# Third chunk's rows from a product on chip, scores ahead of the first gate product, and a new hand-written order, in a fused attention, expert and mixer kernel

## The chip, the cores and the metric

The kernel runs on one core of a Trainium2 chip. The metric is the device time of one execution in microseconds (us), the median of several runs. TensorE is called PE here, VectorE DVE, ScalarE ACT, GpSimd POOL, and SyncE SP; SP issues nearly all DMAs.

## What is computed

Three layers, one behind the other, on a batch of 2 with 768 positions, 8 heads of 40 and so 320 columns:

```
# 1. a gated linear recurrence (per batch and head)
m_new = max(f[t] + m, i[t]); C = exp(f[t] + m - m_new) * C + exp(i[t] - m_new) * outer(v[t], k[t])
n     = exp(f[t] + m - m_new) * n + exp(i[t] - m_new) * k[t]
y[t]  = sigmoid(o[t]) * (C @ q[t]) / max(|n . q[t]|, 1)
# 2. four experts of causal attention (head size 64), the best two of four per position, weighted
a = softmax(mask(q @ k.T / 8)); out += weight * (a @ v @ wo)
# 3. a mixer: over positions (768 -> 256 -> 768), then over columns (320 -> 1536 -> 320)
u = x + (relu(x.T @ w_tok1) @ w_tok2).T;  out = u + relu(u @ w_ch1) @ w_ch2
```

## The kernel before

The recurrence is worked in 12 chunks of 128 positions (6 of each batch, n = 0 to 11). A first stage on DVE scans the gates of all heads at once: `gates` (L322 on) makes running sums `fl`, then `av`, a running maximum `mt`, and from these, with ACT's help, the split operands `lt` and, in `m_ends`, `msp`, both in the tile `ms`. It does so in three pieces of two chunks. The gates of the first two chunks come by two DMAs (`gates0`), the others by one of 512 KB (`gates1`), which SP issues as its fourth.

For each chunk, `m_rows` lays the row maxima of four heads into a tile `rt` of 128 x 512 (four such tiles; chunks from 2 on use the last two in turn). Chunks 0 and 1 get theirs by a product of `msp` with a selection out of `smlt`, on DVE as one multiplication or on ACT as four activations; the later chunks fill the tile once with ones and zeros (`copy`) and then have SP write rows into it by two DMAs out of `msp`. `m_products` multiplies `lt` with `rt` on the PE, with a mask product (`negb`, `identb`) in front for the first four chunks; `m_gates` takes the exponential on ACT into `e`; `m_whole` makes the score products `kv` x `kv`; `m_scores` multiplies both on DVE into `e` (L587) and makes `vs` for the carried state. `m_carry` makes the carry's weights `w` by a product with `mc`, `m_intra` multiplies `e` and `w` with values and carried state (`cb`), divides (`dn`, `x`), and transposes x into `xt`, `m_update` renews the state `cc`, `cb`. Every second chunk is then projected (`p_qk`, `p_v`) with the weights `wh`, `wl`. Attention (`a_scores` to `a_tail`) and the mixer follow.

Nothing is scheduled at run time: the table `ORDER` (L45 on) is a list of some 1,500 numbers. A number x runs the next step of part x // 5 on engine "PAVGS"[x % 5]; a step states what must have been done and which buffers it takes. A negative number -k puts k fillers on the PE (products of `still`, zeros in bf16 of 128 columns). Each engine executes its instructions in that order and waits for what they need, so the table sets the order on every engine and, for copies and multiplications that several engines can do, which one does them. The 8 PSUM banks are handed round.

Of the kernel before, what the change touches and what calls it, by code (L numbers as in the profile page):

```python
# [39 lines left out]
EARLY = 4  # L40
STOP = -1000
# [14 lines left out]
    937, 422, 524, 895, 187, 508, 432, 900, STOP, 560, 917, 187, 440, 488, 936, 896, 387, 440, 561, 901, 1482, 530,  # L56
# [1175 lines left out]
```

## Time and profile before

| | us |
|---|---|
| median of 3 runs | 334.23 (334.22 to 334.96) |
| the profiled execution | 334.46 |
| its span, first to last instruction | 332.7 |

| engine | busy us | share of the span |
|---|---|---|
| PE | 326.1 | 98% |
| DVE | 243.1 | 73% |
| ACT | 179.4 | 54% |
| POOL | 43.3 | 13% |

A busy share is an average over stages: DVE is nearly always busy up to about 180 us and half idle behind, the PE is busy throughout. Products on the PE overlap, so that each one's duration is longer than the step from its start to the next one's start.

### The profile page before, as it was taken

To read this page: it belongs to the slowest core of one execution; us is meant where nothing else is said; L and a number is where in the kernel's file an instruction comes from. 1 tells how busy PE (TensorE), PEld (TensorE's weight loads), DVE (VectorE), ACT (ScalarE), POOL (GpSimd) and SP (SyncE) were. 2 spreads that over 40 slices of the span, in tenths; PEclk is the share of its full clock that TensorE was granted. 3 is DMA by queue.
4 is the path that set the end of the run, shared out by engine and by line. 5 is a ranking of instruction groups with operands and counts; after the bars stand their busy time and mean duration, and the time that the engine had idled before them with its cause. 6 is when DMAs were issued, how large, how long until landed. Compare 5 with 4: busy or idle time off the path is not lost.

```text
span 332.7 us, 7751 instructions
## 1 busy us (share of the span) xinstructions
PE 326.1 (98%) x3034; PEld 293.8 (88%) x3034; DVE 243.1 (73%) x674; ACT 179.4 (54%) x453; POOL 43.3 (13%) x82
## 2 busy tenths in 40 slices
PE   8999999999989999999999999999999999999995
PEld 7779989898888989988899899999889989889985
DVE  4999999999999999999997636543535886411413
ACT  7997769787938886678685513311213442211110
POOL 4232443031421000011120010000000000000000
PEclk9999999999999999999999999999999999999999
DMA  7962844540300354121011502000101200100302
GB/s 228 394 225 97 304 157 153 216 155 13 144 0 3 128 175 144 49 87 41 2 42 48 164 12 89 0 0 2 47 0 41 87 1 2 39 2 0 104 16 79
DMA packets 10300, 29.05 MB, mean 87 GB/s; under 512 B 1272, under 2 KB 3224, under 8 KB 10264
## 3 DMA queue, kind: packets, MB, share of 16 engines
q1 hardware_dynamic: 10120, 28.54, 24.8%
q8 instruction: 24, 0.39, 0.5%
q14 instruction: 12, 0.10, 0.1%
q10 hardware_dynamic: 144, 0.02, 0.0%
HBM read 26.50 MB, written 1.97 MB: 86 GB/s over the span
## 4 chain that ended last, share of the span: by engine, by line
PE 57%; DVE 32%; ACT 4%; issue 3%; DMA 2%; SPq 0%; POOL 0%; DVEq 0%; POOLq 0%; ACTq 0%
PE bank L195 52%; DVE am L864 3%; PE bank L881 3%; DVE e L587 3%; DVE tf L477 3%; DVE tf L474 2%; DMA gt<-in_dram 2%; DVE cw L219 1%; DVE w L222 1%; DVE tf L472 1%; DVE xt L677 1%; ACT am L870 1%; DVE x L222 1%; PE bank L625 1%; DVE q L763 1%
## 5 line engine op out<-in xcount | busy, mean ns | idle before, releaser
L195 PE MATMUL bank<-ut,cw 128*128 128x512 f32 x288 | 72.4, 395 | 0.0
L195 PE MATMUL bank<-cw,h 128*128 128x320 f32 x432 | 70.6, 310 | 0.0
L195 PEld LDWEIGHTS bank<-cw,h 128*128 128x128 f32 x432 | 66.0, 188 | 2.7 <-issue 0.2
L1044 ACT ACTIVATE h<-bank 128x512 fp32r<-128x512 f32 x36 | 21.6, 600 | 78.4 <-PE bank L195 78.3
L195 PEld LDWEIGHTS bank<-ut,cw 128*128 128x128 f32 x288 | 52.6, 188 | 9.8
L1046 DVE SCALAR_TENSOR_TENSOR h<-bank,h 128x512 fp32r<-128x512 f32 x36 | 24.8, 689 | 48.4 <-ACT h L1044 48.4
L870 ACT ACTIVATE am<-am,mn 128x128 f32<-128x128 f32 (+5 forms) x48 | 32.1, 671 | 11.0 <-DVE mn L867 6.6
L864 DVE CUSTOM_DVE_ANT_0 am<-bank,mk 128x384 f32<-128x384 f32 (+3 forms) x64 | 30.6, 500 | 0.8 <-PE bank L195 0.7
L195 PE MATMUL bank<-xt,wh 128*128 128x256 f32 x144 | 26.6, 290 | 0.0
L881 PE MATMUL bank<-ident,am 128*128 128x128 f32 x168 | 24.8, 275 | 0.0
L195 PE MATMUL bank<-ks,q 64*128 64x384 f32 (+2 forms) x192 | 22.4, 343 | 1.1 <-DVE q L763 1.0
L469 ACT ACTIVATE tf<-raw 128x384 f32<-128x384 f32 (+1 forms) x32 | 17.1, 535 | 11.4 <-DVE cw L219 6.0
L216 ACT COPY atr<-bank 128x384 f32<-128x384 f32 (+3 forms) x53 | 22.2, 442 | 2.0 <-PE bank L881 1.9
L195 PEld LDWEIGHTS bank<-xt,wh 128*128 128x128 f32 x144 | 21.8, 189 | 1.0 <-issue 0.2
L195 PE MATMUL bank<-atr,vg 128*64 128x128 f32 x336 | 22.2, 277 | 0.0
L881 PEld LDWEIGHTS bank<-ident,am 128*128 128x128 f32 x168 | 19.4, 140 | 1.8 <-issue 0.3
L195 PEld LDWEIGHTS bank<-atr,vg 128*64 128x64 f32 x336 | 18.4, 137 | 2.1 <-issue 0.6
L195 PEld LDWEIGHTS bank<-ks,q 64*128 64x128 f32 x192 | 15.8, 185 | 4.9 <-DVE q L763 1.2
L477 DVE SCALAR_TENSOR_TENSOR tf<-raw,minus,tf 128x384 uint32<-128x384 uint32 (+1 forms) x32 | 19.1, 595 | 0.2
L474 DVE SCALAR_TENSOR_TENSOR tf<-raw,tf 128x384 uint32<-128x384 uint32 (+1 forms) x32 | 17.5, 556 | 0.3
L1070 DVE TENSOR_TENSOR u<-bank,u 128x320 f32<-128x320 f32 x24 | 11.0, 486 | 8.5 <-PE bank L195 8.5
L587 DVE TENSOR_TENSOR e<-bank,e 128x512 f32<-128x512 f32 x24 | 16.2, 682 | 0.1
(160 smaller groups left out, 601.5 us busy)
## 6 DMA issues: line engine op xcount, KB each, us to landing
kv<-in_dram SPq DMA_DIRECT2D x11, 848.0 KB
raw<-in_dram SPq DMA_DIRECT2D x20, 384.0 KB
raw<-in_dram SPq DMA_DIRECT2D x13, 320.0 KB
os<-in_dram SPq DMA_DIRECT2D x4, 480.0 KB
out_dram<-u SPq DMA_DIRECT2D x12, 160.0 KB
raw<-in_dram SPq DMA_DIRECT2D x3, 386.0 KB
kv<-in_dram SPq DMA_DIRECT2D x1, 512.0 KB
gt<-in_dram SPq DMA_DIRECT2D x1, 512.0 KB
```

What stands on the lines that cost most here:

```text
L195: PE.matmul(o, lt, r, start=first, stop=last)
L216: (A.copy if e == "A" else V.tensor_copy)(o, i)
L469: A.activation(t, w[:, :, 1].bitcast(F32), AF.Copy, scale=2.0 ** -112)
L474: V.scalar_tensor_tensor(u, w[:, :, 0], 29, u, op0=OP.logical_shift_right, op1=OP.bitwise_or)
L477: V.scalar_tensor_tensor(t.bitcast(U32), w[:, :, 1], minus.bitcast(U32), u, op0=OP.bitwise_and, op1=OP.bitwise_or)
L587: V.tensor_mul(EE[n, u], PS[n][u], EE[n, u])
L864: V.tensor_tensor_reduce(a[:, b0 * 128:b1 * 128], s["p", e, ci], mks, -0.125, 3e38, OP.add, OP.min, s["mn"][:, ci, e:e + 1])
L870: A.activation(a[:, 0:w], a[:, 0:w], AF.Exp, bias=s["mn"][:, z, e:e + 1], scale=-1.0, accum_out=s["sm"][:, 0, e:e + 1])
L881: PE.transpose(pt[:, k - b0], a[:, k * 128:(k + 1) * 128], ident)
L1044: A.activation(h[0], p1, AF.Relu)
L1046: V.scalar_tensor_tensor(h[1], p1, 0.0, f32(h[0]), op0=OP.max, op1=OP.subtract)
L1070: V.tensor_add(uo(b, i), ACC[h, n // 4][n % 4], uo(b, i))
```

## The change

Three rules are changed, and the table is a new one. The constant `DIRECT = 3` lets chunk 2 get its rows by the product too, so that the DMAs begin with chunk 3. `m_products` waits for the chunk before it by its own mark ("pd") and no longer by the count that the carry's product shares. `m_whole` no longer waits for the gate product of its chunk, only for the score products of the chunk before, so that scores can stand in front. A step of `a_tail` waits for its neighbour's. The program gains one line, so that every line number behind it is one higher.

```diff
+DIRECT = 3
 ORDER = [
-    12, -19, 65, 4, 12, 256, 196, 12, 16, 17, 11, 61, 65, 12, 111, -49, 65, 12, 12, 86, 49, 9, 109, 12, 71, 12, 16,
+    4, 12, 256, -19, 65, 12, 12, 65, 16, 17, 11, -18, 75, 12, 9, 12, 61, 112, 12, 65, 147, 115, 115, 71, 115, 12,
...
     def m_rows(n):
         b, c = divmod(n, NCH)
         free = (("mg", n - 2),) if n > 3 else ()
-        if n > 1 and (n < 4 or c < 2):
+        if n >= DIRECT and (n < DIRECT + 2 or c < 2):
             yield on("AV", "sml", *free)
             copy(plan.eng, rt(n), sel(n, True))
-        if n > 1:
-            yield on("S", ("msp", c), *free, *((("rti", n - 1),) if n > 2 else ()))
+        if n >= DIRECT:
+            yield on("S", ("msp", c), *free, *((("rti", n - 1),) if n > DIRECT else ()))
...
-                yield on("P", "idb", *((("mg", n - 1),) if n else ()), take=["bank"])
+                yield on("P", "idb", *((("pd", n - 1),) if n else ()), take=["bank"])
...
-        yield on("P", ("kv" if n else "kq", n), ("pd", n), take=["bank"] * 2)
+        yield on("P", ("kv" if n else "kq", n), *((("ps", n - 1),) if n else ()), take=["bank"] * 2)
...
-        yield on("AV", take=["big"] * (1 - i % 2))
+        yield on("AV", *((("up", b, i - 1),) if i % 2 else ()), take=["big"] * (1 - i % 2))
```

By the built programs, the fillers go from 80 (19, 49, 2, 2, 8) to 55 (19, 18, 11, 3, 2, 1, 1), POOL makes 19 `vs` instead of 14 and 7 `x` instead of 3, and DVE that many fewer.

On the PE, at the first gate products, behind the 49 fillers (`rt_86` and `rt_87` hold the rows of chunks 0 and 1, `kv_72` is the first chunk's load), stood:

```order
L195 MATMUL bank<-rt_86,ms 128x512 x2
L195 LDWEIGHTS identb
L195 MATMUL bank<-negb,identb 128x512
L195 MATMUL bank<-kv_72 128x128 x8
L195 LDWEIGHTS identb
L195 MATMUL bank<-negb,identb 128x512
L195 MATMUL bank<-rt_87,ms 128x512 x2
```

There stands now, on the PE behind 18 fillers:

```order
L196 MATMUL bank<-kv_72 128x128 x8
L196 MATMUL bank<-rt_86,ms 128x512 x2
L196 LDWEIGHTS identb
L196 MATMUL bank<-negb,identb 128x512
L196 LDWEIGHTS identb
L196 MATMUL bank<-negb,identb 128x512
L196 MATMUL bank<-rt_87,ms 128x512 x2
L196 MATMUL bank<-rt_87,mc 128x512
```

The scores of chunk 0 are now in front of its gate product, and the carry product of chunk 1 follows its gate product at once. (A row with x8 on two halves of the array is 16 records in the profile.)

On DVE, from the end of the first gates' piece to the second piece (`mp` belongs to the carry, the first `gt` scan to the gates of chunks 2 and 3), stood:

```order
L420 SCALAR_TENSOR_TENSOR mp<-mpf,smlt,mp 128x1
L327 SCALAR_TENSOR_TENSOR gt<-zz,gt 128x256
L219 TENSOR_TENSOR gt<-gt 128x256
L331 TENSOR_SCALAR zz<-gt 128x2
L334 SCALAR_TENSOR_TENSOR mh<-zz,mh,gt 128x256
L222 TENSOR_TENSOR vs<-kv_72,e 128x164
L587 TENSOR_TENSOR e<-bank,e 128x512
```

There stands now, on DVE at the same place:

```order
L421 SCALAR_TENSOR_TENSOR mp<-mpf,smlt,mp 128x1
L223 TENSOR_TENSOR rt_87<-smlt,ms 128x512
L328 SCALAR_TENSOR_TENSOR gt<-zz,gt 128x256
L599 TENSOR_SCALAR mc<-smlt,mp 128x128
L220 TENSOR_TENSOR gt<-gt 128x256
L332 TENSOR_SCALAR zz<-gt 128x2
L223 TENSOR_TENSOR vs<-kv_72,e 128x164
L335 SCALAR_TENSOR_TENSOR mh<-zz,mh,gt 128x256
L588 TENSOR_TENSOR e<-bank,e 128x512 x2
```

DVE now makes the rows of chunk 1 in front of the second gates' scan, and `mc` behind it, both ACT's work before.

On ACT, from the first rows on (`hs` is a half of the split operands, `w` the carry's weights), stood:

```order
L379 ACTIVATE rt_86<-ms,smlt 128x128 x4
L379 ACTIVATE rt_87<-ms,smlt 128x128 x4
L548 ACTIVATE e<-bank 128x512 x2
L352 ACTIVATE hs<-mh,smlt 128x256
L337 ACTIVATE hs<-gt,smlt 128x256
L596 ACTIVATE mc<-smlt,mp 128x128
L548 ACTIVATE e<-bank 128x512 x2
L606 ACTIVATE w<-bank 128x512
```

There stands now, on ACT at the same place (`rt_88` holds the third chunk's rows):

```order
L380 ACTIVATE rt_86<-ms,smlt 128x128 x4
L549 ACTIVATE e<-bank 128x512 x4
L353 ACTIVATE hs<-mh,smlt 128x256
L338 ACTIVATE hs<-gt,smlt 128x256
L607 ACTIVATE w<-bank 128x512
L380 ACTIVATE rt_88<-ms,smlt 128x128 x4
L405 ACTIVATE os<-os 128x960
```

The rows of chunk 1 have left ACT, the exponentials of chunks 0 and 1 stand in a row in front of the second piece, and the third chunk's rows are made behind it. On SP, the first of the weight loads (`raw`, 386 KB) stood in front of the second half of the first `kv`, and stands behind the third `kv` now; in front of the fourth `kv` SP issues the loads of the second half of the first kv, kv 1, os, kv 2, wo, two raw and the rows of chunk 3, where it was raw, kv, kv 1, os, kv 2, raw, the rows of chunk 2, os.

## Rows read from the trace of the kernel before

**Rows 1.** The page's busy times: engine, us, share of the span, instructions

```profile
PE 326.1 (98%) x3034; PEld 293.8 (88%) x3034; DVE 243.1 (73%) x674; ACT 179.4 (54%) x453; POOL 43.3 (13%) x82
```

**Rows 2.** Busy us by stage: from:to, length, PE, weight loads, DVE, ACT, POOL

```profile
8.08:21.63 13.55, 12.97 (x193) 9.77 (x191) 12.96 (x33) 12.81 (x32) 4.10 (x7) 1.00 0.90 346
21.63:192.00 170.37, 168.83 (x1992) 152.90 (x1992) 160.46 (x496) 127.11 (x343) 33.30 (x55) 1.00 0.31 107
192.00:329.30 137.30, 137.28 (x784) 124.94 (x782) 65.19 (x134) 33.69 (x67) 2.14 (x3) 1.00 0.08 26
```

**Rows 3.** Timeline of the PE, start: start us, us, what, count [idle before]

```profile
3.99 4.16 PE L195 MATMUL bank<-still 128*128 128x128 bf16 x49
8.08 0.50 PE L195 MATMUL bank<-rt,ms 64*128 64x512 f32 x2
...
8.83 1.16 PE L195 MATMUL bank<-kv 40*128 40x128 f32 x16
...
16.72 0.61 PE L195 MATMUL bank<-still 128*128 128x128 bf16 x8
...
18.86 1.13 PE L195 MATMUL bank<-kv,e 128*64 128x41 f32 x32
...
20.79 0.50 PE L195 MATMUL bank<-rt,ms 64*128 64x512 f32 x2
21.63 1.16 PE L195 MATMUL bank<-kv 40*128 40x128 f32 x16 [0.34 <-DMA kv<-in_dram]
```

**Rows 4.** Fillers by form, up to 6.5 us and from 6.7 to 8.05: count, busy us, mean ns

```profile
L195 PE MATMUL bank<-still 128*128 128x128 bf16 x43 | 5.0, 314 | 1.0 <-POOL still L239 1.0
L195 PE MATMUL bank<-still 128*128 128x128 bf16 x26 | 1.7, 225 | 0.0
```

**Rows 5.** Timeline of DVE, the second gates' scan and chunk 1's last e product

```profile
8.32 0.69 DVE L327 TENSOR_TENSOR_SCAN gt<-zz,gt 128x256 f32<-128x256 f32 x1 [0.89 <-DMA gt<-in_dram]
...
17.35 0.68 DVE L587 TENSOR_TENSOR e<-bank,e 128x512 f32<-128x512 f32 x1
```

**Rows 6.** Timeline of ACT, the rows and exponentials of chunks 0 and 1

```profile
6.35 2.45 ACT L379 ACTIVATE rt<-ms,smlt 128x128 fp32r<-128x128 f32 x8
8.70 1.05 ACT L548 ACTIVATE e<-bank 128x512 f32<-128x512 f32 x2
...
11.67 1.05 ACT L548 ACTIVATE e<-bank 128x512 f32<-128x512 f32 x2
```

**Rows 7.** Timeline of SP, the fourth kv's issue

```profile
14.09 1.07 SPq L258 DMA_DIRECT2D kv<-in_dram  x1
```

**Rows 8.** The page's DMA issues: os, and the loads of 320 KB with wo

```profile
raw<-in_dram SPq DMA_DIRECT2D x13, 320.0 KB
os<-in_dram SPq DMA_DIRECT2D x4, 480.0 KB
```

**Rows 9.** Stages as in rows 2; the last column is what the DMA moved, GB/s

```profile
0.00:5.00 5.00, 3.96 (x31) 3.23 (x32) 2.32 (x7) 3.01 (x6) 3.76 (x17) 1.00 0.54 157
5.00:8.30 3.30, 3.30 (x44) 3.16 (x41) 1.69 (x6) 3.04 (x9) 0.00 (x0) 1.00 0.97 334
8.30:21.60 13.30, 12.75 (x191) 9.58 (x189) 12.93 (x33) 12.56 (x31) 4.10 (x7) 1.00 0.90 345
```

**Rows 10.** Timeline of the PE, the first chunk's transposes in front of 20.79

```profile
20.37 0.38 PE L625 MATMUL bank<-ident,x 128*128 128x128 f32 x2
20.59 0.27 PE L626 MATMUL bank<-ident,rem 128*128 128x128 f32 x1
```

**Rows 11.** Timeline of the PE, the one long wait of the middle part

```profile
92.43 1.15 PE L195 MATMUL bank<-ks,q 64*128 64x256 f32 x11 [0.96 <-DVE q L763]
```

**Rows 12.** Instructions of x and of e by engine: count, ns least/median/most, first and last start

```profile
L222 DVE TENSOR_TENSOR x<-os,dn x9: 481/491/929, 21.2 to 114.7; 128x320 f32<-128x320 f32 x9
L222 POOL TENSOR_TENSOR x<-os,dn x3: 722/723/922, 17.4 to 81.2; 128x320 f32<-128x320 f32 x3
L554 POOL TENSOR_SCALAR_AFFINE_SELECT e<-e x16: 627/634/746, 31.1 to 98.6; 128x512 f32<-128x512 f32 x16
```

More of the change, by code (lines that the diff above doesn't have):

```diff
@@ L40 @@
 EARLY = 4
+DIRECT = 3
 STOP = -1000
 ORDER = [
[11 rows of a table removed]
-    937, 422, 524, 895, 187, 508, 432, 900, STOP, 560, 917, 187, 440, 488, 936, 896, 387, 440, 561, 901, 1482, 530,
[67 rows of a table removed]
[12 rows of a table added]
+    503, 31, 910, 440, 387, STOP, 530, 508, 490, 561, 1487, 186, 315, 441, 551, 187, 187, 536, 951, 320, 442, 1482,
[66 rows of a table added]
 ]
@@ L530, in m_products @@
             for u in range(2):
-                yield on("P", "idb", *((("mg", n - 1),) if n else ()), take=["bank"])
+                yield on("P", "idb", *((("pd", n - 1),) if n else ()), take=["bank"])
                 PD[n].append(bank([128, 4, L]))
                 mm(PD[n][u], identb, negb[:, None, :].to_broadcast([128, 4, L]), True, False)
-        yield on("P", ("rt", n), ("lt", c), *((("mg", n - 1),) if n else ()), take=["e"] * 2 if early else ["bank", "e"] * 2)
+        yield on("P", ("rt", n), ("lt", c), *((("pd", n - 1),) if n else ()), take=["e"] * 2 if early else ["bank", "e"] * 2)
         if not early:
```

154 rows, old and new, of the table ORDER are left out of this document.

## The prediction

> **What bounds the kernel now.** I read the page's head first [rows 1]: the TensorE (PE) is counted busy in 98% of the span. Then the busy times by stage [rows 2]. From 192.00 to 329.30 the PE is busy 137.28 of 137.30 us and DVE less than half: nothing waits there, so a change of order can gain only by what it does before 192. From 21.63 to 192 the PE is busy 168.83 of 170.37 us and DVE 160.46: the PE is the limit, and DVE, at 94%, is close behind. From 8.08 to 21.63 DVE, with 12.96 of 13.55, and ACT are full, and the PE waits for them. Its busy count hides this, since some of what it runs there are fillers, products of zeros: the timeline of the PE shows 49 before the first gate product at 8.08 and 8 at 16.72 [rows 3]; two groups of 2 stand between them.
>
> So the reader needs two things: when the PE reaches a place after which it runs without pause, and how long its own work takes from there.
>
> **A place to compare at.** The PE's work in front of the fourth chunk's score products (kv, 21.63 [rows 3]) is the same set in both orders, fillers apart: gate products, scores and carries of three chunks, the first two chunks' values, one transpose, and the fourth chunk's gate product. I therefore work out when the changed kernel gets there.
>
> **The start, step by step.** The second gates land as before; DVE's wait for them ends at 8.32 [rows 5]. The rows of chunk 0 come from four of the eight activations that start at 6.35 and take 2.45 us together [rows 6]: the fourth ends at about 7.6. The PE started their product at 8.08, since 49 fillers stood in front of it: 0.4 us lost. Now 18 fillers end at 3.99 + 18 x 0.107 = 5.9 (0.107 is the 0.314 us filler's start-to-start before 6.5 us: 3.99 to 6.5 holds 24). Then the first scores need the first part of kv. Its landing isn't in the trace, since nothing waited for it. It is queued in front of the second gates' 512 KB, and 0.79 MB have to pass up to its end: at the first 5 us' 157 GB/s that is 5.0 us, and at the latest 8.3 less 512 KB at 334 GB/s, 6.7 [rows 9]. I take 6.2. The 16 scores took 1.16 us at 8.83 [rows 3], and end at 7.4 now, between 7.1 (they can't start before the fillers' 5.9) and 7.9. So they cost nothing or, at the late end, 0.3, since the rows of chunk 0 come at 7.6; behind the gate product they would cost their 1.16.
>
> The rows of chunk 1 move from ACT, where the last of them ended at 8.80, to one DVE product in the 0.89 us that DVE waited in front of 8.32 [rows 5]: about 0.68 us, as long as its other product of 512 columns at 17.35, and so hidden by that wait. If the gates land 0.2 us earlier, the cover is gone and it costs 0.2. ACT is free of four activations, so the exponentials of chunk 0 start at 8.2 instead of 8.70, and those of chunk 1 at 9.2 instead of 11.67 [rows 6].
>
> From 8.32 DVE is the chain. Up to the second product e of chunk 1 it ran 24 instructions before, to 17.35 + 0.68 = 18.03 [rows 5], of which the first and the last stand there, 0.40 us each. The new order has 23 up to there, of the same kinds: it leaves out a vs, the third maximum scan and a cc sum (moved to POOL or behind) and puts in two short ones, mc and a dc of 4 columns. One fewer is 0.4; as the scan is a long one (0.69 for the one at 8.32) and the two are short, up to 0.7. I take 0.6: that product ends at 17.4. The third chunk's rows were two DMAs out of msp into a tile filled before. Now they are four ACT activations, half of the 2.45 us [rows 6], 1.2, behind the msp of chunks 2 and 3. They push os's tanh, the cb copies and chunk 2's exponentials on ACT back by as much as ACT saved earlier: I count zero, and 1.2 if the cb copies, for which the PE's carry products wait, come too late. Two DMAs leave SP's queue; the fourth chunk's two come up to their place, so the load of the fourth kv behind them is issued at about 14.1, as before [rows 7].
>
> Behind DVE's 17.4 the PE ran, from the values of chunk 1 at 18.86 to the fourth gate product at 20.79 [rows 3], 1.93 us of values, masks and transposes. The new order has the same there, with one carry product and three fillers more (0.3 and 0.3, estimated from 0.50 for a pair of 512 columns at 20.79, and from the fillers' steps), and then the gate product, 0.4: 17.4 + 0.1 + 1.93 + 0.6 + 0.4 = 20.4. The fourth kv has to be there, too. Its landing ended the PE's wait at 21.63. In front of it 160 KB less are queued now: wo (320) instead of the second os (480) [rows 8]. At the mean rate from 8.3 to 21.6, 345 GB/s [rows 9], it lands 0.47 earlier, at 21.15. So the start gains 0.5 if that rate holds, and 1.2 if the landing is no limit; I take 0.8, in the middle, since the DMA engines were not full up to the end.
>
> **The PE's own work.** The PE runs its products in three forms: full ones (128*128), two column halves (128*64) and two row halves (64*128, 40*128). A step from one form to another costs extra: the transposes of 20.37 (two) and 20.59 (one) [rows 10] follow each other at 0.11 us a product, but from the last, at 20.59, to the row halves at 20.79 [rows 3] it is 0.20. So 0.09 for each change of form. Counted in the order of products there are 87 changes of form before and 74 now; behind the fourth scores 71 and 60. 11 x 0.09 = 1.0 us less. It may be worth nothing where the PE waits anyway, so 0 to 1.0; as the PE is busy in 99% of that stretch [rows 2] I take 1.0.
>
> **Waits behind 21.63.** The new order has other ones, which no row shows. Before, the PE's unbusy time there was 1.5 us, 0.96 of it one wait for the low half of q at 92.43 [rows 11]. The new order can save all of it or have as much again: -1.5 to +1.5, and I take 0. In its favour: DVE gives away four x, 2.0 us at 0.49 [rows 12], five vs and four casts of q and ks, and takes on one row product, one os and a few more atr copies, so that its 160 us become fewer.
>
> **The sum.** -0.8 - 1.0 + 0 = -1.8 us. The profiled execution took 334.46 (span 332.7 and 1.76 around it): 332.7. The median was 0.23 lower than this execution: 332.4.
>
> **Rivals.**
> 1. The start's gain is eaten. The fourth kv lands as late as 21.3, and waits behind it use up the changes of form, since DVE is 94% busy: -0.3 to -0.8 in all, 333.4 to 333.9 for the median. For it: the PE waited for this very landing. Chance 0.24, with the cases from there to a small loss.
> 2. More than forecast: the new order also loses the wait at 92.43 and gets the full 1.2 at the start: -3.0 to -3.7, 330.5 to 331.2. Chance 0.10.
> 3. Slower, through POOL. It gets four more x (7 instead of 3). One takes 0.72 us there against 0.49 on DVE [rows 12], and can queue behind a mask of e, 0.63. The chain reciprocal, x, transpose, projection grows by 0.23 to 0.86 at each, and DVE stands still where less than that lies between its reciprocal and its use. At the fifth chunk only two short minima (am) do. If more than half of the seven are uncovered and in front of products that the PE needs next, 4 x 0.86 = 3.4 us come on top of -1.8: 335.8. Against it: at the others a product e or another of 512 columns, 0.6 us or more, and something else lies between. Chance 0.10.
> 4. The clock. Before, fillers took 314 ns up to 6.5 us and 225 ns from 6.7 on [rows 4]: PE went from 1.2 to 2.4 GHz there, after having run nearly without pause from 1.04. (The page's clock reads 1.00 throughout and doesn't show it.) Now there is a pause from 5.9 to about 6.2 in front of the scores. If the clock rises later for it, the PE's products of the next microseconds take up to twice as long (314 against 225 ns for one, but two to one in their steps: 24 up to 6.5, and 25 from there to 8.08, in 2.5 and 1.5 us). Some 3 us of them lie between 7.6 and 12, of which DVE's chain hides one: 0.8 to 2 on top, 333.2 to 334.4 for the median. The Trainium skill's page TensorE: Matmul & The Clock Gate (What's actually happening) has it that the slow level is the default and activity lifts it, so that fewer fillers can cost; no run here shows the case yet. Chance 0.08.
>
> **How the numbers follow.** The forecast has 0.48 (331.3 to 333.2), rival 1 0.24, rival 2 0.10, rival 3 0.10, rival 4 0.08. 0.3%, 1.0 us, is about what a measurement of this kernel tells from no change: faster means below 333.2. The forecast and rival 2 are faster, 0.58, with 0.01 of rival 4; rival 1, but for 0.05 of it that ends slower, and the rest of rival 4 are no change: 0.26. Slower is that 0.05 and rival 3: 0.15. The range leaves out the better half of rival 2 and rival 3: 330.8 to 334.9.
>
> **What would show it.** Right: the first gate product at 7.6 to 7.8 with the scores in front of it; the second e of chunk 1 ending at about 17.4; the fourth scores at 20.4 to 21.2; the stretch from there to the last product shorter by about 1 us. Wrong: a PE wait for kv in front of the scores past 7.6; fillers or scores still at the slow level after 7; DVE idle in front of L664 with POOL's x as releaser; PE waits of over 1 us between 30 and 190.

## The result and the profile after

The changed kernel takes 330.62 us, the median of 11 runs (330.19 to 334.02), against 334.38 of 11 runs of the kernel before (333.92 to 335.05): a ratio of 0.9897, with an interval of 0.9874 to 0.992. It is 3.8 us faster, twice the 1.8 of the forecast, and the median lies 0.2 below the low end of the range. One of the eleven runs, the one of 334.02, had a mean TensorE clock of 0.989; the experiment on the scores' place below shows what that likely is.

The profiled execution took 330.19, with a span of 328.4 (before 334.46 and 332.7). The page's head, with the busy times of [rows 1], and the shares of the chain that ended last, by engine:

```profile
span 328.4 us, 7681 instructions
...
PE 321.6 (98%) x3009; PEld 290.9 (89%) x3009; DVE 239.3 (73%) x665; ACT 180.3 (55%) x453; POOL 49.7 (15%) x92
...
PE 83%; DVE 11%; DMA 3%; issue 1%; SPq 0%; ACT 0%; POOL 0%; DVEq 0%
```

PE is still the bound: it is counted busy for 4.5 us less, and the span is 4.3 shorter. Two of the stages of [rows 2], in the same columns:

```profile
8.08:21.63 13.55, 13.52 (x213) 10.46 (x212) 13.41 (x34) 13.13 (x31) 5.55 (x10) 1.00 1.02 405
21.63:192.00 170.37, 169.43 (x1986) 155.05 (x1986) 156.87 (x485) 129.18 (x348) 38.83 (x62) 1.00 0.31 102
```

In the first stage PE and DVE do more in the same 13.55 us, and the DMA moves 405 GB/s in place of 346. In the second, PE's unbusy time is 0.94 us (170.37 less 169.43), in place of 1.54. The start of PE's timeline, to be laid beside [rows 3]:

```profile
5.89 1.16 PE L196 MATMUL bank<-kv 40*128 40x128 f32 x16 [0.77 <-DMA kv<-in_dram]
7.67 0.50 PE L196 MATMUL bank<-rt,ms 64*128 64x512 f32 x2 [0.61 <-ACT rt L380]
...
13.26 0.48 PE L196 MATMUL bank<-rt,ms 64*128 64x512 f32 x2
...
16.69 1.13 PE L196 MATMUL bank<-kv,e 128*64 128x41 f32 x32
...
19.66 1.16 PE L196 MATMUL bank<-kv 40*128 40x128 f32 x16
```

The first scores start at 5.89 and stand in front of the first gate product (7.67, before 8.08). The third chunk's gate product stands at 13.26. The values of chunk 1 start at 16.69 (18.86), and the fourth scores, the place of comparison, at 19.66 (21.63), with no wait for their operands. SP issues their load at 13.29 (14.09):

```profile
13.29 0.34 SPq L259 DMA_DIRECT2D kv<-in_dram  x1
```

DVE, to be laid beside [rows 5]:

```profile
7.35 0.69 DVE L223 TENSOR_TENSOR rt<-smlt,ms 128x512 fp32r<-128x512 f32 x1
7.95 0.69 DVE L328 TENSOR_TENSOR_SCAN gt<-zz,gt 128x256 f32<-128x256 f32 x1
...
15.96 0.68 DVE L588 TENSOR_TENSOR e<-bank,e 128x512 f32<-128x512 f32 x1
```

The second chunk's rows fill the place of the wait, the scan starts at 7.95 without one, and the second e of chunk 1 ends at 16.64 (18.03).

Between the two profiled executions, 1.97 us of the gain lie in front of the fourth scores. From there to the start of the last product it took 307.34 us before and takes 305.00 now: another 2.34. PE's waits, summed over the whole span by what they waited for (us in total, times, longest):

```profile
PE bank L196 <- POOL still L240: 1.0, 1, 1.0
PE bank L196 <- DMA kv<-in_dram: 0.8, 1, 0.8
PE bank L196 <- ACT rt L380: 0.6, 1, 0.6
PE bank L196 <- DVE up L959: 0.3, 1, 0.3
```

The first three lie before 7.7 us. Behind the fourth scores the longest is 0.3; the one of 0.96 for q [rows 11] is gone, and three of 0.2 to 0.3 stand there.

### The profile page after: what moved, and what is told of

Read it like the earlier page. It is cut to its first block, busy times and chain, and to the rows that moved or that the text cites. A ratio compares the mean times of both kernels' runs of the same rounds, so it can differ in the third digit from the quotient of the medians.

```text
span 328.4 us, 7681 instructions
## 1 busy us (share of the span) xinstructions
PE 321.6 (98%) x3009; PEld 290.9 (89%) x3009; DVE 239.3 (73%) x665; ACT 180.3 (55%) x453; POOL 49.7 (15%) x92
## 3 DMA queue, kind: packets, MB, share of 16 engines
HBM read 26.50 MB, written 1.97 MB: 87 GB/s over the span
## 4 chain that ended last, share of the span: by engine, by line
PE 83%; DVE 11%; DMA 3%; issue 1%; SPq 0%; ACT 0%; POOL 0%; DVEq 0%
PE bank L196 75%; PE bank L882 5%; DMA os<-in_dram 2%; PE bank L626 1%; DVE e L588 1%; DVE am L865 1%; PE bank L907 1%; DMA gt<-in_dram 1%; PE bank L627 1%; DVE w L223 1%; DVE u L1071 1%; DVE x L664 0%; DVE xt L678 0%; DVE ms L340 0%; DVE gt L328 0%
## 5 line engine op out<-in xcount | busy, mean ns | idle before, releaser
L217 ACT COPY atr<-bank 128x384 f32<-128x384 f32 (+3 forms) x49 | 20.1, 440 | 3.4 <-PE bank L882 3.2
L196 PE MATMUL bank<-ks,q 64*128 64x384 f32 (+2 forms) x192 | 21.6, 341 | 0.3 <-DVE up L959 0.3
L220 DVE TENSOR_TENSOR cw<-tf,cw 128x320 fp32r<-128x320 f32 (+2 forms) x36 | 15.2, 423 | 1.2 <-ACT cw L481 0.9
```

The costliest lines, as they stand in the source:

```text
L196: PE.matmul(o, lt, r, start=first, stop=last)
L217: (A.copy if e == "A" else V.tensor_copy)(o, i)
L220: (V if e == "V" else G).tensor_sub(o, a, b)
```

## The experiments

In the diffs, numbers are steps of the hand-written order, and a negative number is so many fillers.

### The same kernel again

No edit. 

> The changed kernel as it is, a second profiled execution, beside the others of this comparison. In nine traces so far the gates' landing, the landing of the first scores' operands and the moment at which TensorE's spacing falls from 0.107 to 0.056 us scatter by 0.9, 0.9 and 2.9 us between executions. Theory (the start scatters by what the transfers and the clock do, the part behind it does not): fourth scores anywhere from 19.6 to 21.5, from them to the last product 304.9 to 305.1, time 330.2 to 331.5. Rival (the start of the changed kernel is fixed by its order): fourth scores 19.6 to 19.8.

Measured: 330.65 (330.14 to 331.21), ratio 0.988 (0.9859 to 0.99). PE and DVE in its trace:

```profile
6.72 1.16 PE L196 MATMUL bank<-kv 40*128 40x128 f32 x16 [1.66 <-DMA kv<-in_dram]
...
20.07 1.16 PE L196 MATMUL bank<-kv 40*128 40x128 f32 x16
```

```profile
8.10 0.69 DVE L328 TENSOR_TENSOR_SCAN gt<-zz,gt 128x256 f32<-128x256 f32 x1 [0.17 <-DMA gt<-in_dram]
```

The first operands land 0.8 later than in the first trace and the scores wait for them, the scan waits 0.17, and the fourth scores start 0.4 later. From there it takes 305.07, and 305.03 to 305.10 in three more traces with this rest, whose fourth scores start between 20.69 and 23.75 (the two with the scores behind and the one with the weight load in front, below). So the start scatters by some tenths with what the DMA does, and the new rest doesn't: a start has to be judged by timed runs, the new rest can be read from one trace.

### The two halves exchanged

All engines' steps up to the fourth scores come from one kernel, the rest from the other. Here the program is that of before, with its rules, and the order alone is edited.

```diff
-ORDER = <the kernel before's>
+ORDER = <the kernel before's up to 270, the fourth scores> + <the changed kernel's steps that are left>
```

> The start of the kernel before with the rest in the changed kernel's order. Theory (start and rest add up): fourth scores at 21.4 to 21.8, time 331.8 to 332.5. Rival (the later order only gains because the start is early): 333.5 to 334.5. Rival (all of the gain is in the later order): 330.4 to 331.0.

Measured: 331.57 (331.34 to 331.67) against 334.42, ratio 0.9916 (0.9902 to 0.9929). The fourth scores start at 21.09, and from there it takes 304.92, as in the changed kernel. The rest in its new order needs no early start: by the medians it is worth 2.85 of the 3.8 us, and the start 0.95 (331.57 against 330.62; by the ratios, 0.9916 against 0.9897, 0.6). In single traces the start looks larger, since that of before was a late one.

The other way round, new start and old rest, in the changed kernel's program, with `a_tail`'s rule of before: 

> The start of the changed kernel (everything up to the fourth chunk's score products, on all engines) with the rest in the order of the kernel before. Between the two profiled runs the start gave 2.0 us and what lies behind the fourth scores 2.3 us. Theory (TensorE is busy to the end, so what is gained at the start is still there at the end): fourth scores at 19.5 to 20.0, time 332.2 to 332.8 against 334.4 of before. Rival (the later waits for other engines eat the start's gain, and all of the gain is in the later order): 334.0 to 334.6.

Measured: 335.97 (334.45 to 336.81), ratio 1.0054 (1.0041 to 1.0068), slower than before; both expectations missed. The profiled execution took 334.45. PE and DVE:

```profile
19.82 1.16 PE L194 MATMUL bank<-kv 40*128 40x128 f32 x16
22.96 0.79 PE L194 MATMUL bank<-cb,w 128*64 128x82 f32 x16 [1.98 <-DVE w L221]
```

```profile
21.73 0.48 DVE L353 SCALAR_TENSOR_TENSOR ms<-mh,smlt,hs 128x256 fp32r<-128x256 f32 x1 [0.73 <-ACT hs L351]
22.13 0.68 DVE L221 TENSOR_TENSOR w<-w,kv 128x512 f32<-128x512 f32 x1
```

The start's gain of 1.8 is there at 19.82 and is gone at 22.96: the old rest has the carry product next, and DVE starts w only at 22.13, behind an e and two ms, of which the second waits 0.73 for ACT. So PE's early start is worth something only with a rest whose first operands are early, too. The four other runs took 335.83 to 336.81 at a mean clock of 0.995, the profiled one had 0.999; what made that difference isn't in a trace. This hybrid is no clean measure of the start, since the old rest also finds DVE's queue in another state.

### The one long wait of before

```diff
-1050, 818, 1512, 782, 773, 841, 582, 778
+1050, 818, 582, 1512, 782, 773, 841, 778
```

582 is DVE's subtraction for the low half of q, which gives a bank free; 1512 a weight step, and 782 a small copy. The kernel is that of before. 

> The kernel before with one step moved on DVE: the subtraction that gives the query bank free (91.70 in its trace) stands ahead of the 0.92 us weight step and the 0.42 us copy that are ahead of it. TensorE's wait of 0.96 us at 92.43 should go. Theory (a wait of TensorE in the middle shows at the end in full): 333.4 to 333.8. Rival (the next wait takes it back): 334.2 to 334.6.

Measured: 333.36 (333.04 to 333.77), ratio 0.9971 (0.996 to 0.9983): 1.06 us less. PE runs through the place of [rows 11] without a wait:

```profile
90.49 1.84 PE L193 MATMUL bank<-ks,q 64*128 64x384 f32 x18
92.47 1.16 PE L193 MATMUL bank<-kv 40*128 40x128 f32 x16
```

At the kv scores (92.47, before 93.30) it is 0.83 ahead, and at the end of the last product 0.99. Of the 0.83, 0.16 comes from the start: this trace has its fourth scores at 20.87 (21.63), 0.76 earlier with the same order, but its fifth at 35.15 (35.31).

```profile
20.87 1.12 PE L193 MATMUL bank<-kv 40*128 40x128 f32 x16
22.44 0.79 PE L193 MATMUL bank<-cb,w 128*64 128x82 f32 x16 [0.45 <-ACT e L546]
```

So the old rest eats an early start of its own kernel, too. One step moved two places up in DVE's queue gives more than a quarter of what the whole change gives, and a wait of the middle part does show at the end.

### What a change of form costs

```diff
         p1 = bank([128, 512])
+        mm(p1[:, 0:128], still, still, True, True)
```

The second kernel has `still[0:64], still[0:64]` there. 

> The changed kernel with one product more ahead of each of the 36 channel products: 128 rows by 128 columns of zeros, bf16, into the bank that the channel product then overwrites, in the same form of the array (128x128) as what stands before and behind it. Nothing of the result changes. Both theories: 36 times 0.056 us, the spacing of the same product among the fillers at full clock, 2.0 us more than the changed kernel (332.6).

> As the run with 36 more products of the full form, but each reads 64 rows only (form 64x128), so that TensorE changes its form 72 times more. Theory (a change of form costs about 0.09 us wherever it stands, as the forecast took it): 72 times 0.09, 6.5 us more than with the full form, about 339. Rival (what the forecast read as a change of form is something else, such as the first product on a new operand): the same time as with the full form, 332.6.

Measured: 335.35 (334.52 to 337.95) with the full form, ratio 1.0043 (1.0014 to 1.0071), and 343.13 (342.77 to 346.25) with the half form, 1.0283 (1.0228 to 1.0338). One of the 36 places in each trace, full and half:

```profile
241.10 0.60 PE L194 MATMUL bank<-cw,h 128*128 128x320 f32 x3
241.54 0.23 PE L194 MATMUL bank<-still 128*128 128x128 bf16 x1
241.58 2.11 PE L194 MATMUL bank<-ut,cw 128*128 128x512 f32 x8
```

```profile
244.37 0.60 PE L194 MATMUL bank<-cw,h 128*128 128x320 f32 x3
244.91 0.23 PE L194 MATMUL bank<-still 64*128 64x128 bf16 x1
245.06 1.20 PE L194 MATMUL bank<-ut,cw 128*128 128x512 f32 x4
```

By the medians of the 36 places, the start of the extra product comes 0.09 later in the half form (0.241 behind the one before, 0.150 in the full form), and the next product 0.118 later (0.157 and 0.039): 0.104 for a change of form, close to the forecast's 0.09. The difference of the two times, 7.8 us over 72 changes, gives 0.108. The Trainium skill's page TensorEngine Tiling (Array Packing), Key Properties, says that changing the tiling mode drains TensorE; the traces agree in so far as each change costs time, and put the number to it; a drain itself they don't show.

The full form was missed: 4.7 us for 36 products, 0.13 each, where the fillers' spacing had given 0.056. The price of a filler in a row of fillers isn't its price between large products. By the starts in the trace, 0.08 of it lies behind the extra product, in the step from the first large product to the second (0.31, in place of 0.23 in the changed kernel). A likely reason, only argued, is that the next weights (PEld, 0.19 us for 128 rows) no longer load beside a product long enough to hide them.

### The scores in front of the gate product

```diff
-65, 16, 17, 11, -18, 75, 12, 9, 12, 61, 112, 12, 65, 147
+65, 16, 17, 11, -18, 12, 9, 12, 61, 112, 12, 65, 75, 147
```

75 is the first chunk's scores, the last 65 its gate product. 

> The changed kernel with the first chunk's score products behind its gate products, as before, and nothing else moved. Theory (in front they fill 0.9 us in which TensorE would idle, behind they stand on the path to the products with the carry and of the second chunk): fourth scores 0.5 to 1.0 later, 331.1 to 331.7. Rival (TensorE waits for DVE behind them anyway, the place is free): 330.5 to 330.8.

Measured: 334.14 (331.06 to 334.41), ratio 0.9969 (0.9947 to 0.9992): most of the change's gain is lost, far more than either theory had. PE in its trace, and then two stages in the columns of [rows 2]:

```profile
7.60 0.50 PE L194 MATMUL bank<-rt,ms 64*128 64x512 f32 x2 [2.13 <-ACT rt L378]
7.93 1.81 PE L194 MATMUL bank<-kv 40*128 40x128 f32 x16
...
23.75 1.16 PE L194 MATMUL bank<-kv 40*128 40x128 f32 x16
```

```profile
7.60:11.00 3.40, 3.40 (x22) 2.23 (x22) 2.50 (x7) 1.08 (x2) 0.62 (x1) 0.56 1.01 378
11.00:14.00 3.00, 3.00 (x16) 1.72 (x14) 2.40 (x5) 2.53 (x6) 0.89 (x2) 0.50 1.02 421
```

PE stands for 2.13 us, and the granted clock (behind the number of POOL) is 0.56 and 0.50 up to 14: the level of 1.2 GHz. The scores take 1.81 us instead of 1.16. To tell the clock from the scores' place, the fillers of before were put back:

```diff
-65, 16, 17, 11, -18, 12, 9, 12, 61, 112, 12, 65, 75, 147
+65, 16, 17, 11, -49, 12, 9, 12, 61, 112, 12, 65, 75, 147
```

> The first chunk's score products behind its gate products, and 49 fillers (as before) in place of 18 ahead of the gate products, so that TensorE works until the gate product is ready. With 18 fillers TensorE stood 2.1 us and the trace shows 0.107 us spacing again until 13.8. Theory (most of what that run lost is the clock, which falls back when TensorE stands): no slow stretch behind 7.5, fourth scores 20.2 to 21.3, time 331.2 to 332.0 and no execution near 334. Rival (the loss is the score products' place on the path): 333.0 to 334.4 as with 18 fillers.

Measured: 331.19 (331.11 to 331.36), ratio 0.9896 (0.9876 to 0.9915), as expected. PE, and the first of the two stages:

```profile
3.98 4.16 PE L194 MATMUL bank<-still 128*128 128x128 bf16 x49
8.08 0.50 PE L194 MATMUL bank<-rt,ms 64*128 64x512 f32 x2
...
20.69 1.16 PE L194 MATMUL bank<-kv 40*128 40x128 f32 x16
```

```profile
7.60:11.00 3.40, 3.40 (x35) 2.18 (x33) 3.40 (x9) 1.61 (x4) 0.71 (x1) 1.00 1.01 397
```

So of 3.5 us lost by the scores' place with 18 fillers (by the medians), 3.0 go with the clock, and 0.5 is the place itself. The ten executions with 18 fillers say the same: six took 334.0 to 334.4, at a mean clock of 0.989 or 0.990 (one of 0.998), three 332.7 to 332.9 at 0.993 or 0.994, and the one at 1.000 took 331.06, about as long as those with 49 fillers. In front, the scores do what the fillers did, keep PE at work, with work that counts. It may also say why the changed kernel's start is less safe: its one run at clock 0.989, as long as most runs without scores in front, is likely one in which their operands landed late. That run has no trace.

### The first weight load

```diff
-... 11, -18, 75, 12, 9, 12, 61, ...  102, 200, 49, 54
+... 11, -18, 75, 12, 49, 9, 12, 61, ...  102, 200, 54
```

49 is SP's load of 386 KB, 9 that of the first chunk's values. 

> The changed kernel with the first weight load (386 KB) back ahead of the first chunk's value load in SyncE's queue, as it stood before. Theory (that load, right behind the gates, shares the engines with them and holds them up, and its move is why the scan started at 7.95 without a wait): a wait of DVE for the gates comes back in front of the scan, which starts at 8.2 to 8.4, and the fourth scores start 0.3 to 0.4 later, 330.9 to 331.1. Rival (the gates land when they land; the wait went for another reason): scan at 7.95, 330.5 to 330.7.

Measured: 331.53 (331.34 to 331.96), ratio 0.9912 (0.9894 to 0.9929): by the medians 0.9 slower than the changed kernel, some 0.5 more than the theory had, and by the ratios 0.5, with intervals that overlap. In its trace the fourth scores start at 21.46. DVE:

```profile
8.81 0.69 DVE L326 TENSOR_TENSOR_SCAN gt<-zz,gt 128x256 f32<-128x256 f32 x1 [0.87 <-DMA gt<-in_dram]
...
10.67 0.33 DVE L221 TENSOR_TENSOR vs<-kv,e 128x164 f32<-128x164 f32 x1 [0.58 <-DMA kv<-in_dram]
```

The wait for the gates is back, and one for the values comes behind it. But the kernel with the scores behind and 18 fillers, which has that load late, also waited for its gates:

```profile
8.85 0.69 DVE L326 TENSOR_TENSOR_SCAN gt<-zz,gt 128x256 f32<-128x256 f32 x1 [0.90 <-DMA gt<-in_dram]
```

In the ten traces with the load late the scan starts at 7.93 to 8.85, in the four with it in front at 7.97 to 8.81. So the order in SP's queue is worth the 0.5 to 0.9 us that the times show, but that it moves the gates' landing isn't shown, and the scan at 7.95 of the first trace is partly luck.

### The third chunk's rows by the DMA

```diff
-DIRECT = 3
+DIRECT = 2
...
-147, 133, 196, 102, 200, 49, 54
+147, 133, 196, 102, 49, 54, 199, 200
```

196 is now the copy ahead of the two DMAs, 199 the DMAs, 200 the gate product on them. The fifth chunk's copy is left out. 

> The changed kernel with the third chunk's rows by the DMA, as before: SyncE issues them (1.46 us) as soon as its end values are there (11.7), behind the two weight loads, and TensorE's gate product on them stands where it stands now (13.3). Theory (the product on chip is what lets that gate product stand so early): the rows land near 15, TensorE waits 1 to 2 us there, the fourth chunk's load is issued up to 1.5 us later, time 331.5 to 332.6. Rival (other products were late anyway, the transfer is hidden): 330.5 to 331.0.

Measured: 337.23 (337.03 to 337.85), ratio 1.0079 (1.006 to 1.0098), 6.6 us slower than the changed kernel; the theory had the direction and a fifth of the size. SP, PE and a stage in the columns of [rows 2]:

```profile
13.21 2.76 SPq L369 DMA_DIRECT2D rt<-ms  x4
```

```profile
17.85 0.59 PE L194 MATMUL bank<-rt,ms 64*128 64x512 f32 x2 [3.79 <-DMA rt<-ms]
18.37 1.53 PE L194 MATMUL bank<-vs,kv 128*64 128x41 f32 x16
```

```profile
17.80:25.00 7.20, 7.15 (x85) 6.43 (x85) 2.87 (x5) 3.95 (x8) 1.61 (x3) 0.54 0.58 225
```

The rows are there at 17.85, 4.6 us after their issue began; up to then PE stands for 3.79, and then the clock is at 0.54 up to 25: 16 products that take 0.92 in the changed kernel take 1.53. The old order didn't pay this, as it had that gate product at 17.54. The product on chip, which costs ACT 1.28 us, is what lets the order be what it is. Only this one place for the DMAs was tried, behind two weight loads; one in front of those loads wasn't.

### Two attempts to go further

> The changed kernel with five small edits to its order: the 3 fillers ahead of the third chunk's scores and the 1 ahead of the fourth's are left out, and three DVE steps change places so that a bank or an operand that TensorE waits for comes earlier (waits of 0.26 us at 91.9, 0.28 at 135.9 and 0.28 at 150.0). Changes of form 74 to 71. Theory (TensorE is the bound to the end, so every wait and change that goes is time): 3 changes at 0.10, 4 fillers at 0.06 and waits of 0.8, 1.3 us less, 329.2 to 329.7. Rival (the waits come back a step later): 330.3 to 330.8.

In the diff, 1022 and 1072 are the low halves of up and of yh, 1522 and 1712 weight steps, 1252 a mask step, 857 and 852 the low halves of ks and q, and 1317 the softmax sums.

```diff
-... 12, 221, -3, 210, 132 ...  260, 233, -1, 270
+... 12, 221, 210, 132 ...  260, 233, 270
-1072, 1022   ...  1522, 1210, 1525, 725, 1714, 1252   ...  1712, 857, 1273, 852, 1784, 1270, 1300, 1286, 1696, 1317
+1022, 1072   ...  1210, 1525, 725, 1714, 1252, 1522   ...  1712, 1317, 857, 1273, 852, 1784, 1270, 1300, 1286, 1696
```

Measured: 330.92 (330.59 to 331.41), ratio 0.9888 (0.9869 to 0.9908), no different from the 330.65 beside it. From the fourth scores it took 305.58, 0.5 more. The waits at 91.9 and 135.9 went, but one of 0.27 came at 95.69, and at 150.12 PE waits for a bank:

```profile
150.12 1.12 PE L194 MATMUL bank<-wo,yh 128*128 128x320 f32 x6 [0.75 <-ACT tf L468]
```

```profile
149.32 0.66 DVE L762 TENSOR_TENSOR ks<-bank,ks 128x512 fp32r<-128x512 f32 x1
```

DVE's ks, which gives that bank free, ends at 149.98: the softmax sums had been put ahead of it. (The step named as releaser is the one that came last by the records; the one that ends just before PE starts is ks.) The second attempt puts ks, q and the sums, in this order, ahead of the weight step, and the product w (377) ahead of x (302):

```diff
-303, 302, ... 896, 301, 377   ...  1522, 1210, ... 1252   ...  1295, 1712, 857, 1273, 852, 1784, ... 1696, 1317
+303, 377, 302, ... 896, 301   ...  1210, ... 1252, 1522   ...  1295, 857, 852, 1317, 1712, 1273, 1784, ... 1696
```

> The changed kernel with other edits to DVE's order alone, at four waits of TensorE behind the fourth scores: the product w stands ahead of x, for which DVE waits 0.46 us at 34.3 (wait 0.34 at 36.9); a weight step stands behind the mask step that gives a bank free (0.28 at 135.9); and the two subtractions that give banks free and the sums of the softmax stand ahead of two weight steps of 1.28 us (0.28 at 148.5 and 0.28 at 150.0). The fillers are as in the changed kernel. Theory (a wait that goes and whose place no later step inherits is time): from the fourth scores to the last product 303.9 to 304.4 in place of 305.0 to 305.1, time 329.5 to 330.0. Rival (the next wait takes it back, as in the first attempt, where a bank that came free later cost 0.7): 304.8 to 305.3, 330.4 to 330.9.

Measured: 331.38 (330.34 to 334.04), ratio 0.9931 (0.9908 to 0.9954), no gain; 305.20 from the fourth scores. At 149.60 the trace is 0.4 ahead of the changed kernel's, as meant. Then the weight loads of PE wait for banks that DVE's atr copies give free:

```profile
150.43 0.53 PEld L194 LDWEIGHTS bank<-ks,q 64*128 64x128 f32 x6 [0.28 <-DVE atr L215]
151.37 0.52 PEld L194 LDWEIGHTS bank<-ks,q 64*128 64x128 f32 x5 [0.40 <-DVE atr L215]
```

and at 152.25 it is 0.24 behind. In the changed kernel DVE is busy 72.48 of the 75 us from 103 to 178:

```profile
103.00:178.00 75.00, 74.86 (x797) 69.00 (x794) 72.48 (x231) 56.63 (x156) 11.56 (x17) 1.00 0.26 80
```

What is put forward in such a queue puts something else back, and there PE needed that, too. I found no version that beats the changed kernel.

## Why the prediction came out as it did

The direction and the mechanism held: PE is the bound, and what it loses less at the start and behind the fourth scores is the gain. But the likeliest case, 332.4, was not what came. What came has the size of rival 2, "more than forecast", and one of its two parts: the wait at 92.43 goes. The other, the full 1.2 at the start, the timed runs don't bear out; the rest of the size comes from behind the fourth scores, and a part of that is in no term of the prediction. Point by point:

- **The first scores and the first gate product.** Right: operands at 5.89 and 6.72 in two traces (taken 6.2, 5.0 to 6.7), the gate product at 7.67 (7.6 to 7.8).
- **DVE's chain.** Too cautious: the second e of chunk 1 ended at 16.64 instead of 17.4. "The second gates land as before" failed by 0.37 in the first trace and 0.22 in the second, both within the scatter of the landing; moving the weight load, which the step didn't price, is worth 0.5 to 0.9 by its own experiment. The rest, 0.4, is the chain from the scan on: 8.7 us instead of 9.1.
- **The landing of the fourth kv.** The step that kept the start small: 21.15 by the old mean rate of 345 GB/s, with the load issued at about 14.1. It was issued at 13.29, the DMA moved 405 in that stretch, and the fourth scores at 19.66 didn't wait.
- **The start.** -0.8 taken (0.5 to 1.2). By the medians of the exchanged halves 0.95, by the ratios 0.6. The two traces, with 1.97 and 1.56, overstate it, as the start scatters: the fourth scores come at 20.87, 21.09 and 21.63 in three traces with the old start (21.20 in the mean) and at 19.66 to 20.34 in six with the new one (19.94). That gives 1.3; the term itself was about right.
- **Changes of form.** -1.0 taken, 11 at 0.09. The price measured 0.104, so about -1.1. That these 11 changes gave it is argued from the price and the count; they weren't put back one by one.
- **The waits behind.** The term that was mis-sized: 0 taken of -1.5 to +1.5. The rest gave 2.85 by the medians and 2.34 between two traces. Less 1.1 for the changes of form, 1.2 to 1.7 are left. One part is the wait of 0.96 for q, worth 1.06 when it is taken away alone. For this one no average over "other waits" was needed: the trace of before shows which DVE step gives the bank free, that a weight step of 0.92 and a copy of 0.42 stand ahead of it, and the new order could have been read at that place. But waits of 0.2 to 0.3 came in its place, so that PE's unbusy time fell by only 0.6 in all, from 1.54 to 0.94. So 0.6 us between the traces, and 1.1 by the medians, stays without a term: it lies in steps between products in which PE is counted busy. The bound of 1.5 took PE's unbusy time for all that there was to save. What shortened those steps, dearer changes of form than 0.104 or waits that the count hides, no experiment took apart.
- **Rows of the third chunk, counted zero.** Right for ACT: the gate product on those rows didn't wait for them in the first trace and waited 0.16 in the second. But the step compared the four activations with the two DMAs in SP's queue, and missed what the product allows: that gate product at 13.26 instead of 17.5.
- **Rival 1** (the start eaten by later waits) is what the old rest does with the new start, in one wait of 1.98. The new rest doesn't: it takes 304.9 to 305.1 us from fourth scores at 19.66 to 23.75. **Rival 3** (POOL's x) cost DVE one wait of 0.46, at 34.80. **Rival 4** (the clock) is real, with a larger price than the 0.8 to 2 given: about 3, but ten of the changed kernel's eleven runs, with a mean clock of 0.999 or 1.0, didn't pay it.

## What to carry to other kernels

Where one engine is the bound, look at each of its long waits singly: find the step that ends it, what stands ahead of that step in its queue, and whether anyone needs that first; moving one step two places gave 1.06 us here. Waits of 0.3 us in a stretch where the other engine is 97% busy came back elsewhere, twice. At the start, work that counts in front of a wait is better than fillers, but whatever stands there must last until the next operand lands; and a start is judged by timed runs, since traces with the same start were 0.7 to 0.8 us apart at the fourth scores.

## What the runs showed of the hardware

The time at which PE's clock rises to 2.4 GHz isn't fixed by the order. The same 18 fillers at 4 us took 1.17 us in the second trace of the changed kernel and 2.08 in the first attempt to go further, whose order is the same up to there, 0.056 and 0.107 us from one to the next:

```profile
3.90 1.17 PE L196 MATMUL bank<-still 128*128 128x128 bf16 x18
```

```profile
4.00 2.08 PE L194 MATMUL bank<-still 128*128 128x128 bf16 x18
```

Where fillers end before the next operand is there, this costs nothing; with work in their place it likely would, which no run tests. That a stand of 2.13 us early in the kernel could bring the clock back to 1.2 GHz, and that this would cost more (3.0 us) than the stand itself, I had not expected; the Trainium skill's page TensorE: Matmul & The Clock Gate (What's actually happening) has the slow level as the default that activity releases, and the trace agrees. Not every such stand did it: 1.66 us in front of the scores in the second trace of the changed kernel, and 1.98 in that of the new start with the old rest, left a mean clock of 0.999.
